# Padded score rows, filler matmuls, a later due time for MLP units and another engine for some subtractions in a fused attention and MLP kernel

## The chip, the cores and the metric

The kernel runs on one core of one Trainium2 chip. The metric is device time in microseconds of a whole execution. The core has a matrix engine (TensorE, PE in the profile, with PEld for its weight loads), a vector engine (VectorE, DVE), a scalar engine (ScalarE, ACT), a general engine (GpSimd, POOL) and a queue that issues the transfers (SyncE, SP).

## What is computed

Attention with a bias of running sums, then two MLPs, all in float32 (B, H, S, D = 4, 8, 576, 64; 2304 tokens of 512 numbers):

```python
scores = q @ k.T / 8 + minimum(-(cum_i - cum_j), 0)   # cum: running sum of relu(s); causal mask
attn = softmax(scores) ; x = attn @ v                 # per batch and head, 576 x 576
h = x @ w_in ; g = h * clip(h + 3, 0, 6) / 6 ; x2 = g @ w_out        # 512 -> 2048 -> 512
m = maximum(maximum(x2 @ w1, x2 @ w2), x2 @ w3) ; out = m @ w_out2   # 512 -> 768 -> 512
```

## The kernel before

Most products are made of three products of float32r numbers: each operand is kept as a rounded high part and a low part (the difference), and `three` (L474 to L476) multiplies high by high, high by low and low by high. Only the first batch's attention is different: its scores and values are multiplied as plain float32, with one instruction in the program that the trace shows as two records.

The order of the work is made in Python before anything is built. `Flow` is a planner: every strand of work is a generator that asks for an engine with a cost in the planner's own microseconds (`mm(n)` is n/2400 + 0.003, and a plain float32 matmul is asked for at `4 * mm(n)`), for a buffer (`Stock`) or for an event. Whoever has the lowest rank gets the engine next, and instructions are issued to the engines' queues in the order in which the planner gave them out. An engine then works in that order on the chip: an instruction that waits holds up all behind it on its queue. After each piece of work that isn't chained, the strand goes on only after a latency (0.2 us for PE, `LATENCY`).

The stages, by the span: the first batch's attention (8 heads; the 128-row blocks of queries 0 and 1 of every head first, then blocks 2 to 4), about 10 to 125 us; the other three batches' attention up to about 355 us, with units of the first MLP between (`hidden1`: `ps_h<-x,w`; `reduce1`: `ps_x<-gt,w`); the rest of the first MLP up to about 684 us; the three products of the second MLP (`ps_j`) up to 882 us; and the last product (`ps_o`) from 882 us to the end. Before the first scores, `setup` (L556) makes `WARM` = 20 matmuls of the 128 x 128 identity with itself.

A block of scores of the first batch goes through `slot` (L806): a matmul whose contracted rows are the 64 numbers of a head and one row for the bias, `tiles[0][0:D + 1, ...]`, so 65 rows; VectorE adds the mask and takes the minimum (L853); ScalarE takes the exponential (L861); TensorE transposes (L883, `pt`); ScalarE copies (L392); and `average` (L915, `px`) multiplies by the 64 columns of the values. The tiles `qt` and `kt` are three pairs of buffers, set up in `staged` (L627 to L635), where GpSimd writes ones into two rows.

The first MLP's unit for a stretch of tokens starts when its `x` is there: for the first batch when it is made, for the others when the transfer that `load_xs` (L1027 to L1043) issues has landed by the planner's reckoning. `hidden1` asks with a rank behind all of attention, so its units fill places that are left.

In the last stage each of 84 right-hand operands (7 combinations of 12 sets) is made of a combination (VectorE, L1183), a rounding to the high part (ScalarE or VectorE, L367, L369) and a subtraction for the low part (L373), which the planner gives to GpSimd or VectorE, whichever takes it first: `hidden_form` (L1544) calls `split_form` (L1177), and that `minus`. The planner treats VectorE and GpSimd operations on SBUF alone as exclusive of each other (`Held`).

Of the kernel before, what the change touches and what calls it, by code (L numbers as in the profile page):

```python
# [9 lines left out]
F32 = mybir.dt.float32  # L10
# [25 lines left out]
NG2 = 3 * NJ // 2  # L36
NG3 = NJ // 2
KEPT = 2
WARM = 20
ORDER = 0  # L40
MOE = 160
AFTER = 8
TINYS = 10
NDM = 1
AFTER_FIRST = 5
AHEAD, BEHIND, PREP = 0, 10, 4
# [70 lines left out]
class Flow:  # L117
    LATENCY = {"PE": 0.2, "DVE": 0.13, "ACT": 0.15, "POOL": 0.08, "SP": 0.0}

    def __init__(self):  # L120
        self.agenda, self.n, self.now = [], 0, 0.0
        self.free = {e: 0.0 for e in self.LATENCY}
        self.ready = {e: [] for e in self.LATENCY}
        self.dma = 0.0
        self.port = 0.0
        self.cur = None
        self.live = set()

# [51 lines left out]
    def dispatch(self, engine):  # L180
        ready = self.ready[engine]
        while ready and self.free[engine] <= self.now + 1e-9:
            passed, chosen = [], None
            while ready and chosen is None:
                one = heapq.heappop(ready)
                if one[5]:
                    continue
                if isinstance(one[3], Held) and self.port > self.now + 1e-9:
                    passed.append(one)
                else:  # L190
                    chosen = one
            for one in passed:
                heapq.heappush(ready, one)
            if chosen is None:
                return
            _, _, th, cost, chained, taken = chosen
            taken.append(engine)
            self.free[engine] = self.now + cost
            if isinstance(cost, Held):
                self.port = self.now + cost  # L200
                for other in ("DVE", "POOL"):
                    if other != engine:
                        self.at(self.port, lambda other=other: self.dispatch(other), ORDER)
            later = 0.0 if chained else self.LATENCY[engine]
            th.t = self.now + cost + later
            self.at(self.free[engine], lambda: self.dispatch(engine), ORDER)
            self.step(th, engine)

    def landing(self, nbytes):
        ev = Event(self)  # L210
# [79 lines left out]
def attn_moe_moe2(ctx, tc, q, k, v, s, w_in, w_out, w1, w2, w3, w_out2, out):  # L290
# [262 lines left out]
    attention_done = event()  # L553
    finished = [0]

    def setup():  # L556
        make_identity(nc, ident)
        pool.memset(above, 0.0)
# [68 lines left out]
    def staged(z, first=False):  # L627
        if (z, first) not in joined:
            joined[z, first] = qt, kt = tuple(
                qp.tile([P, 2, S], F32 if first else F32R, tag=f"{t}{z}", name=t, bufs=1)  # L630
                for t in ("qt", "kt")
            )
            yield "POOL", pool1(2 * S)
            pool.memset((qt if first else qt.bitcast(F32))[D:D + 2], 1.0)
        return joined[z, first]  # L635

    def first_pairs():
# [168 lines left out]
    def slot(i, item, tiny):  # L806
# [5 lines left out]
        if soon:  # L812
            z, *tiles = yield early[part_of(b, c), p]
            o = c * P - UCUT[part_of(b, c)][0]
            passes = [(tiles[0][0:D + 1, j, o:o + n], tiles[1][0:D + 1, j])]
        else:
            passes = [(lhs[:, qs], rhs) for lhs, rhs in (yield h.ready)]
        w = min(S, (c + 1) * P)
# [208 lines left out]
    def load_xs():  # L1027
        for z in range(2):
            for u in range(NU):
# [10 lines left out]
                        x[:, :, cc], x_d[b][:, cc, :, cs].rearrange("l p t -> p l t"), 8 * P * n  # L1040
                    )
                yield d
                x_ready[z, u].set((x, xi))  # L1043

    def hidden1():
        for z in range(2):
# [127 lines left out]
    XFS, TMP, MF = (stock() for _ in range(3))  # L1174
    STAGE = {n: stock() for n in RIGHT.values()}

    def split_form(hi, src, lo, n):  # L1177
        yield from rounded(hi, src, n, ACT + DVE)
        yield from minus(lo, src, hi.bitcast(F32), n, POOL + DVE)

    def combined(dst, a, b_, op, n):
        yield "DVE", held2(n)
# [360 lines left out]

    def hidden_form(t, name, g, items, raw):  # L1544
        f, home = items[name]
        yield from split_form(f[:, 0], raw, f[:, 1], U1)
        right_ready[t, name, g].set((f, home))

    turn2 = [event() for _ in range(2 * NUNIT + 1)]
# [177 lines left out]
    flow.start(-20, cumulate())  # L1727
    flow.start(-10, first_pairs())
    flow.start(0, issue_slots())
    for f in range(NA):  # L1730
        flow.start(WI_PRIO + WI_STEP * f, decode(w_in[f], W, ("i", f)))
    flow.start(40, late_weights())
# [70 lines left out]
```

## Time and profile before

| | us |
|---|---|
| median of 3 runs | 961.94 |
| the three runs | 958.25, 962.2, 961.94 |
| the profiled execution (one of the three) | 962.2 |
| its span in the trace | 960.4 |
| mean granted clock of TensorE, as a share of 2.4 GHz | 0.961 |

The profile is one execution, taken by the hardware profiler. A row of busy tenths divides the span into 40 equal slices of 24 us; PEclk gives TensorE's granted clock in the same slices in tenths of 2.4 GHz, so that 5 is 1.2 GHz. A row of a group of instructions gives line, engine, operation, what is written and read, shapes (for a matmul the weights as rows*columns, then the moving operand), count, busy time, mean duration, and the engine's idle time just before with what ended it. The ends of matmuls are modelled, so two durations that follow each other can overlap; the spacing of starts is the surer number.

### The profile page before, as it was taken

What the parts mean: (1) busy time and instruction counts of PE and PEld (TensorE: products, weight loads), DVE (VectorE), ACT (ScalarE), POOL (GpSimd) and SP (SyncE); (2) the same over time, 40 slices, a digit from 0 to 9 for tenths busy, and PEclk for the clock granted to TensorE, in tenths of its full rate; (3) what the DMA queues carried; (4) which work ended last, traced back from release to release, by engine and by line L of the source; (5) the groups of instructions that cost most, each with busy time, mean ns of one, the idle gap of its engine ahead of it and who ended that gap; (6) DMA issues with size and microseconds to landing.
All of it is one profiled execution on the core that took longest, in us unless ns stands there. A gap on an engine that the chain in (4) does not pass through costs nothing. (4 is left out here: it accounts for less than half of the span.)

```text
span 960.4 us, 18805 instructions
## 1 busy us (share of the span) xinstructions
PE 937.8 (98%) x6520; PEld 864.7 (90%) x6520; DVE 663.4 (69%) x1606; ACT 477.1 (50%) x1215; POOL 354.3 (37%) x452
## 2 busy tenths in 40 slices
PE   8999999999999999999999999999999999999998
PEld 5545579998999999999999999999999999999888
DVE  5567457778888846885577787762857576666874
ACT  4444577867887745664344444442314232323442
POOL 3353544545645223545253454452000000023552
PEclk7558999999999999999999999999999999999999
DMA  7734376789778326664559688848742121374442
GB/s 200 204 89 113 103 171 163 201 211 252 205 191 229 103 99 218 190 213 135 166 204 322 217 286 298 299 153 283 264 139 63 55 70 36 108 265 122 149 124 74
DMA packets 94878, 167.79 MB, mean 175 GB/s; under 512 B 10144, under 2 KB 60840, under 8 KB 94784
## 3 DMA queue, kind: packets, MB, share of 16 engines
q1 hardware_dynamic: 94784, 166.60, 57.4%
q8 instruction: 51, 0.84, 0.4%
q14 instruction: 43, 0.35, 0.1%
HBM read 96.13 MB, written 49.17 MB: 151 GB/s over the span
## 5 line engine op out<-in xcount | busy, mean ns | idle before, releaser
L474 PE MATMUL ps_h<-x,w 128*128 128x320 f32 (+1 forms) x512 | 159.1, 311 | 4.6 <-DVE g L1075 2.5
L474 PE MATMUL ps_x<-gt,w 128*128 128x320 f32 (+1 forms) x512 | 154.4, 302 | 2.3 <-DVE xf L1150 1.6
L373 POOL TENSOR_TENSOR gt<-g,gt 128x256 fp32r<-128x256 f32 (+1 forms) x107 | 86.9, 812 | 176.5 <-ACT gt L367 175.6
L475 PE MATMUL ps_h<-x,w 128*128 128x320 f32 (+1 forms) x512 | 151.4, 296 | 0.0
L476 PE MATMUL ps_h<-x,w 128*128 128x320 f32 (+1 forms) x512 | 151.2, 295 | 0.0
L475 PE MATMUL ps_x<-gt,w 128*128 128x320 f32 (+1 forms) x512 | 150.7, 294 | 0.0
L476 PE MATMUL ps_x<-gt,w 128*128 128x320 f32 (+1 forms) x512 | 150.5, 294 | 0.0
L475 PE MATMUL ps_j<-xf,wf 128*128 128x288 f32 x432 | 127.9, 296 | 0.0
L476 PE MATMUL ps_j<-xf,wf 128*128 128x288 f32 x432 | 127.6, 295 | 0.0
L474 PE MATMUL ps_j<-xf,wf 128*128 128x288 f32 x432 | 127.5, 295 | 0.0
L832 PE MATMUL ps_s<-kt,qt 66*64 66x288 f32 (+14 forms) x384 | 115.4, 399 | 3.9 <-DMA kt<-c 2.8
L861 ACT ACTIVATE e<-e,tiny 128x384 f32<-128x384 f32 (+4 forms) x160 | 96.0, 600 | 38.5 <-DVE tiny L853 37.2
L1071 ACT ACTIVATE u<-ps_h,half 128x256 f32<-128x256 f32 (+1 forms) x128 | 63.8, 498 | 99.3 <-PE ps_h L476 98.5
L474 PEld LDWEIGHTS ps_h<-x,w 128*128 128x128 f32 x512 | 97.2, 190 | 14.7 <-issue 7.3
L853 DVE CUSTOM_DVE_ANT_0 e<-ps_s,above 128x384 f32<-128x384 f32 (+4 forms) x160 | 76.3, 479 | 44.5 <-PE ps_s L832 42.2
L373 POOL TENSOR_TENSOR mh<-mr,mh 128x288 fp32r<-128x288 f32 x36 | 32.2, 902 | 193.8 <-DVE mh L369 160.4
L1075 DVE SCALAR_TENSOR_TENSOR g<-u,ps_h 128x256 f32<-128x256 f32 (+1 forms) x128 | 57.6, 450 | 62.3 <-ACT u L1071 58.6
L474 PEld LDWEIGHTS ps_x<-gt,w 128*128 128x128 f32 x512 | 96.8, 189 | 3.8 <-DVE xf L1150 1.2
L475 PEld LDWEIGHTS ps_h<-x,w 128*128 128x128 f32 x512 | 97.3, 190 | 0.1
L476 PEld LDWEIGHTS ps_h<-x,w 128*128 128x128 f32 x512 | 97.0, 189 | 0.0
L475 PEld LDWEIGHTS ps_x<-gt,w 128*128 128x128 f32 x512 | 96.4, 188 | 0.1
L476 PEld LDWEIGHTS ps_x<-gt,w 128*128 128x128 f32 x512 | 96.3, 188 | 0.0
(159 smaller groups left out, 2220.2 us busy)
## 6 DMA issues: line engine op xcount, KB each, us to landing
f_d<-wf SPq DMA_DIRECT2D x30, 512.0 KB
wf<-f_d SPq DMA_DIRECT2D x30, 512.0 KB
raw<-in_w_out_dram SPq DMA_DIRECT2D x22, 512.0 KB
kt<-kb SPq DMA_DIRECT2D x72, 144.0 KB
raw<-in_w_dram SPq DMA_DIRECT2D x18, 512.0 KB
x<-x_d SPq DMA_DIRECT2D x28, 320.0 KB
raw<-in_w_in_dram SPq DMA_DIRECT2D x16, 512.0 KB
x<-x_d SPq DMA_DIRECT2D x28, 256.0 KB
```

Source lines behind the costliest of these rows:

```text
L373: (pool if e == "POOL" else vec).tensor_tensor(out=dst, in0=a, in1=b_, op=ALU.subtract)
L474: pe.matmul(ps, lhsT=wh, rhs=xh, start=first, stop=False, skip_group_check=again)
L475: pe.matmul(ps, lhsT=wh, rhs=xl, start=False, stop=False, skip_group_check=again)
L476: pe.matmul(ps, lhsT=wl, rhs=xh, start=False, stop=last, skip_group_check=again)
L832: pe.matmul(o, lhsT=lhs, rhs=rhs[:, lo:hi], start=(x == 0), stop=(x == len(passes) - 1),)
L853: vec.tensor_tensor_reduce(out=e[:n, lo:hi], in0=ps[:n, 0:hi - lo], in1=above[:n, shift + lo:shift + hi], scale=-0.125, scalar=m0, op0=ALU ...
L861: act.activation(e[:n, :w], e[:n, :w], AF.Exp, bias=m0, scale=-1.0, accum_out=r,)
L1071: act.activation(ut, ps, AF.Relu, bias=half, scale=1.0 / 6.0)
L1075: vec.scalar_tensor_tensor(out=g, in0=ut, scalar=1.0, in1=ps, op0=ALU.min, op1=ALU.mult)
```

## The change

- Scores of the first batch: both operands are taken over all 128 rows. The rows behind the 64 numbers are zeroed when the tile pair is first used (VectorE writes `kt[D:]`, GpSimd writes `qt[D:]`), and the row of ones is written after that (one row in place of two).
- `WARM` goes from 20 to 34.
- A new strand `keep_warm` runs until the planner's clock is at 60 us. Whenever the planner has PE at work for less than 0.8 of its last 3.4 us, it asks for PE behind everyone else and issues one 128 x 128 float32 matmul of the identity with itself into whichever of the score, transpose or value PSUM buffers has most free places; the result is not used. Otherwise it looks again 0.2 us later.
- `x_ready` for tokens whose `x` is loaded is set 2.5 us later in the planner, so `hidden1` asks later for those units.
- `hidden_form` gives its subtractions to VectorE alone.

```diff
--- before.py
+++ after.py
@@ -36,11 +36,12 @@
 NG2 = 3 * NJ // 2
 NG3 = NJ // 2
 KEPT = 2
-WARM = 20
+WARM = 34
 ORDER = 0
 MOE = 160
 AFTER = 8
 TINYS = 10
+FILL, FILL_UNTIL, WINDOW = 0.8, 60, 3.4
 NDM = 1
 AFTER_FIRST = 5
 AHEAD, BEHIND, PREP = 0, 10, 4
@@ -123,6 +124,7 @@
         self.ready = {e: [] for e in self.LATENCY}
         self.dma = 0.0
         self.port = 0.0
+        self.worked = []
         self.cur = None
         self.live = set()
 
@@ -196,6 +198,8 @@
             _, _, th, cost, chained, taken = chosen
             taken.append(engine)
             self.free[engine] = self.now + cost
+            if engine == "PE":
+                self.worked.append((self.now, self.now + cost))
             if isinstance(cost, Held):
                 self.port = self.now + cost
                 for other in ("DVE", "POOL"):
@@ -205,6 +209,14 @@
             th.t = self.now + cost + later
             self.at(self.free[engine], lambda: self.dispatch(engine), ORDER)
             self.step(th, engine)
+
+    def activity(self, span):
+        lo, done = self.now - span, 0.0
+        for a, b in reversed(self.worked):
+            if b <= lo:
+                break
+            done += b - max(a, lo)
+        return done / span
 
     def landing(self, nbytes):
         ev = Event(self)
@@ -553,6 +565,22 @@
     attention_done = event()
     finished = [0]
 
+    def keep_warm():
+        while flow.now < FILL_UNTIL:
+            free = max((T, S_, V), key=lambda st: len(st.items))
+            if free.items and flow.activity(WINDOW) < FILL:
+                item = free.items.pop(0)
+                yield "PE", 4 * mm(P), False, 1e9
+                pe.matmul(
+                    make(item, [P, 512], F32, "idle")[:, 0:P], lhsT=ident, rhs=ident,
+                    start=True, stop=True,
+                )
+                free.put(item)
+            else:
+                later = event()
+                later.set(at=flow.now + 0.2)
+                yield later
+
     def setup():
         make_identity(nc, ident)
         pool.memset(above, 0.0)
@@ -630,8 +658,13 @@
                 qp.tile([P, 2, S], F32 if first else F32R, tag=f"{t}{z}", name=t, bufs=1)
                 for t in ("qt", "kt")
             )
+            if first:
+                yield "DVE", held1(2 * S)
+                vec.memset(kt[D:], 0.0)
+                yield "POOL", pool1(2 * S)
+                pool.memset(qt[D:], 0.0)
             yield "POOL", pool1(2 * S)
-            pool.memset((qt if first else qt.bitcast(F32))[D:D + 2], 1.0)
+            pool.memset(qt[D:D + 1] if first else qt.bitcast(F32)[D:D + 2], 1.0)
         return joined[z, first]
 
     def first_pairs():
@@ -812,7 +845,7 @@
         if soon:
             z, *tiles = yield early[part_of(b, c), p]
             o = c * P - UCUT[part_of(b, c)][0]
-            passes = [(tiles[0][0:D + 1, j, o:o + n], tiles[1][0:D + 1, j])]
+            passes = [(tiles[0][:, j, o:o + n], tiles[1][:, j])]
         else:
             passes = [(lhs[:, qs], rhs) for lhs, rhs in (yield h.ready)]
         w = min(S, (c + 1) * P)
@@ -1040,7 +1073,7 @@
                         x[:, :, cc], x_d[b][:, cc, :, cs].rearrange("l p t -> p l t"), 8 * P * n
                     )
                 yield d
-                x_ready[z, u].set((x, xi))
+                x_ready[z, u].set((x, xi), at=flow.cur.t + 2.5)
 
     def hidden1():
         for z in range(2):
@@ -1174,9 +1207,9 @@
     XFS, TMP, MF = (stock() for _ in range(3))
     STAGE = {n: stock() for n in RIGHT.values()}
 
-    def split_form(hi, src, lo, n):
+    def split_form(hi, src, lo, n, engines=POOL + DVE):
         yield from rounded(hi, src, n, ACT + DVE)
-        yield from minus(lo, src, hi.bitcast(F32), n, POOL + DVE)
+        yield from minus(lo, src, hi.bitcast(F32), n, engines)
 
     def combined(dst, a, b_, op, n):
         yield "DVE", held2(n)
@@ -1543,7 +1576,7 @@
 
     def hidden_form(t, name, g, items, raw):
         f, home = items[name]
-        yield from split_form(f[:, 0], raw, f[:, 1], U1)
+        yield from split_form(f[:, 0], raw, f[:, 1], U1, DVE)
         right_ready[t, name, g].set((f, home))
 
     turn2 = [event() for _ in range(2 * NUNIT + 1)]
@@ -1727,6 +1760,7 @@
     flow.start(-20, cumulate())
     flow.start(-10, first_pairs())
     flow.start(0, issue_slots())
+    flow.start(NS, keep_warm())
     for f in range(NA):
         flow.start(WI_PRIO + WI_STEP * f, decode(w_in[f], W, ("i", f)))
     flow.start(40, late_weights())
```

## Rows read from the trace of the kernel before

**Rows 1.** The page: span, busy time, and the clock granted in 40 slices

```profile
span 960.4 us, 18805 instructions
...
PE 937.8 (98%) x6520; PEld 864.7 (90%) x6520; DVE 663.4 (69%) x1606; ACT 477.1 (50%) x1215; POOL 354.3 (37%) x452
...
PEclk7558999999999999999999999999999999999999
```

**Rows 2.** TensorE's instructions in order: start, us, what, [idle before it]

```profile
1.35 6.39 PE L574 MATMUL warm<-ident 128*128 128x128 f32 x40 [1.35 <-POOL ident masks.py:199]
10.52 0.89 PE L832 MATMUL ps_s<-kt,qt 65*128 65x128 f32 x4 [2.78 <-DMA kt<-c]
12.01 1.65 PE L832 MATMUL ps_s<-kt,qt 65*128 65x128 f32 x4 [0.60 <-DVE tiny L853]
```

**Rows 3.** Stretches: length, PE PEld DVE ACT POOL busy (x instructions), clock, DMA share, GB/s

```profile
11.50:12.00 0.50, 0.00 (x0) 0.00 (x0) 0.50 (x4) 0.01 (x1) 0.43 (x1) 0.69 1.46 164
12.00:62.00 50.00, 49.48 (x135) 27.44 (x136) 29.17 (x92) 26.27 (x83) 19.19 (x28) 0.50 0.66 179
62.00:79.70 17.70, 17.70 (x45) 8.60 (x44) 9.04 (x25) 6.26 (x15) 4.63 (x7) 0.50 0.29 81
79.70:84.00 4.30, 4.30 (x19) 1.84 (x18) 2.69 (x5) 2.03 (x6) 2.13 (x3) 0.97 0.40 122
84.00:120.00 36.00, 36.00 (x176) 20.28 (x177) 21.47 (x61) 20.20 (x52) 18.30 (x24) 1.00 0.45 118
882.00:946.00 64.00, 59.48 (x426) 57.97 (x425) 52.95 (x102) 29.96 (x84) 37.20 (x43) 0.97 0.44 135
```

**Rows 4.** TensorE's instructions in order, shortly before the clock rises

```profile
77.53 1.70 PE L883 MATMUL pt<-ident,e 128*128 128x128 f32 x7
79.16 1.13 PE L915 MATMUL px<-e2p,vf 128*64 128x320 f32 x2
```

**Rows 5.** TensorE's instructions in order, from one MLP unit to the next, later

```profile
102.14 0.28 PE L476 MATMUL ps_h<-x,w 128*128 128x256 f32 x1
...
103.57 0.93 PE L883 MATMUL pt<-ident,e 128*128 128x128 f32 x7
104.43 0.75 PE L915 MATMUL px<-e2p,vf 128*64 128x320 f32 x2
...
109.30 0.39 PE L474 MATMUL ps_h<-x,w 128*128 128x256 f32 x1
```

**Rows 6.** VectorE by line, 10 to 84 us: busy, mean ns, idle before, releaser

```profile
L853 DVE CUSTOM_DVE_ANT_0 e<-ps_s,above 128x128 f32<-128x128 f32 (+4 forms) x28 | 12.5, 450 | 21.9 <-PE ps_s L832 21.8
```

**Rows 7.** Stretches around a fall of the clock in the later batches

```profile
216.00:220.00 4.00, 2.96 (x22) 2.20 (x20) 3.87 (x13) 3.82 (x11) 4.00 (x6) 0.99 0.92 220
220.00:224.00 4.00, 3.84 (x17) 3.66 (x18) 2.66 (x12) 2.35 (x7) 0.34 (x1) 0.59 0.93 257
```

**Rows 8.** The warm-up line alone, two records to a matmul: stretches of 1 us

```profile
4.00:5.00 1.00, 1.00 (x7) 1.00 (x6) 1.00 0.90 254
5.00:6.00 1.00, 1.00 (x11) 1.00 (x10) 1.00 1.06 315
```

**Rows 9.** Line 634, whole span: duration ns min/median/max, first and last start

```profile
L634 POOL MEMSET qt<- x6: 1051/1051/1057, 2.4 to 119.1; 2x1152 f32 x6
```

**Rows 10.** TensorE's waits over the whole span: us in total, times, longest

```profile
PE ps_o L475 <- DVE mh L373: 3.4, 3, 1.5
...
PE ps_h L474 <- DVE g L1075: 2.5, 3, 1.4
...
PE ps_o L475 <- POOL mh L373: 1.2, 3, 0.5
```

**Rows 11.** Lines 373 and 1183, 836 to 950 us: duration ns min/median/max

```profile
L373 POOL TENSOR_TENSOR mh<-mr,mh x36: 802/832/1117, 839.1 to 944.8; 128x288 fp32r<-128x288 f32 x36
...
L373 DVE TENSOR_TENSOR mh<-mh x17: 445/451/1071, 891.9 to 943.4; 128x288 fp32r<-128x288 f32 x17
L1183 DVE TENSOR_TENSOR mr<-mr,mh x12: 445/752/1067, 840.0 to 937.0; 128x288 f32<-128x288 f32 x12
```

## The prediction

> **What bounds the kernel now.** The page first [rows 1]: TensorE works in 98% of the span, and the line of the granted clock has one long hole, slices 2 to 4, with 5 where all later slices have 9. So the end is set by TensorE's work and by the clock at which it is done, and any other engine matters where TensorE waits for it. The hole is the first batch's attention, and the stretches give its edges [rows 3]: the clock falls from 2.4 to 1.2 GHz between 11.5 and 12.0 us, is 0.50 in all of 12.0 to 79.7, and 0.97 and 1.00 after that. In those 67.7 us TensorE is busy for 49.48 + 17.70 = 67.2 us: it is slow, not idle. What came before the fall stands in its order of work [rows 2]: 20 warm-up matmuls to 7.74 us, 2.78 us of waiting for the transfer of the bias row, one pair of scores, 0.60 us of waiting for VectorE. That TensorE is what the others wait for in this stretch shows on VectorE [rows 6]: before its score line it was idle 21.9 us from 10 to 84 us, 21.8 of them for TensorE's scores. The rest of the span is full at 2.4 GHz; two late places matter for the last two edits: waits in the last stage and for MLP units [rows 10].
>
> **What a release of the clock is worth.** The spacing of starts gives the ratio of the two levels for the same work. Seven transposes take 79.16 - 77.53 = 1.63 us at 1.2 GHz [rows 4] and 104.43 - 103.57 = 0.86 at 2.4 [rows 5], 1.9 to 1. So the 67.2 us are 35.4 us of work at 2.4 GHz. With 0.9 before 12 us [rows 2] and 4.3 from 79.7 to 84.0 [rows 3], everything that TensorE has done by 84.0 us is W = 40.6 us, from the first score on.
>
> **Does the clock stay up?** Once up, the first batch's own mix keeps it up: from 102.14 to 109.30 us no MLP matmul runs, only the 65-row scores, transposes and 64-column values [rows 5], and the clock of that stretch is 1.00 in the row of 84 to 120 us [rows 3]. The same mix did not raise it in 12 to 62 us. So what must be avoided is the fall, and the fall had idle time before it. WARM gives 14 more matmuls, 28 records; at the rate of the fifth us, 11 records in 1 us [rows 8], that is 2.6 us, so the warm-up ends at 7.74 + 2.6 = 10.3, at the first score's 10.52. The padded rows cost no TensorE time that I can see in a row; the nearest are scores of 128 rows in the later batches, in a float format of their own. For them there is one sign more: in the later batches, after a fall at about 220 us, the clock is back within 4 us [rows 7], not after 67. The zeroing adds three GpSimd operations of about 1.05 us [rows 9] and three on VectorE, before the first score where both have gaps, but for the third pair, which puts about 1 us in front of weight subtractions that nothing waits for yet; 0, with 1 us as the other end.
>
> [...]
>
> **The fillers.** `keep_warm` issues at most one per 0.425 us of the planner's time (0.225 for the matmul, 0.2 latency, both in the code). It starts at the planner's 0, where no real matmul is due, and the planner knows nothing of the warm-up. The first score comes at 10.5 us in the trace, which bounds them at 25; the planner's transfers and VectorE costs are shorter than the traced ones, so I take 18. A filler is two records, 0.19 us at the rate above: 3.4 us behind the warm-up, and the first score starts at 10.3 + 3.4 = 13.7 instead of 10.5 (ends 10.5 and 15.1). This isn't all lost, since the clock holds through it, and scores of pairs 1 to 3 come later than pair 0's. After that, fillers stand where the planner has TensorE below 0.8: mostly the first group (12 to 37 us in the trace, half of it at 2.4 GHz), where no MLP unit can fill. Half of the 47 places in 20 us gives 24, D = 4.6 us. Ends: 0, and 117 places in the remaining 50 us of the planner, 22 us. On the chip they cost only where TensorE isn't waiting anyway; with plain float32 values slower than the planner's cost, most will not fall in idle time. Each waits for the last reader of its buffer, and the scores and transposes behind it on TensorE's queue wait with it.
>
> **What is late next.** VectorE has 29.17 + 9.04 + 2.69 = 40.9 us of work from 12 to 84 [rows 3]; in 13.7 to 61 that would be 0.87 of the time, against 0.60 from 84 to 120. So some waits for it will show: I = 3 us (ends 0 and 11).
>
> **The sum for the first batch.** 13.7 + 40.6 + 4.6 + 3 = 61.9 for the point that is now at 84.0: 22.1 us less.
>
> **MLP units held back.** The longest wait for a unit is on VectorE's gate (2.5 us in three) [rows 10], that is, on a PSUM buffer coming free and not on a loaded x. So no wait that the trace shows is removed; a shift of the order is worth 0, with 2 us on either side. Behind a unit that is issued later wait only its own gate, the GpSimd subtraction and `reduce1`.
>
> **Low halves on VectorE.** In 882 to 946 us TensorE is idle 64 - 59.48 = 4.5 us [rows 3], nearly all waits for these low halves, 3.4 on VectorE's and 1.2 on GpSimd's [rows 10]. There are 43 on GpSimd in this stretch. Alone a VectorE one takes 0.45 us and a GpSimd one 0.80; beside each other VectorE's combinations take up to 1.07 [rows 11]. VectorE's 102 operations take 52.95 us now; at 0.45 and less they would take 46 or less, so moving 43 in at 0.37 to 0.45 adds 16 to 19 and gives back 7 to 12: 57 to 65 us of work in 64. I take 58, a few waits gone: -1 us. Ends: -6 (all waits and a short fall of the clock there, 0.97), and +7 if VectorE becomes the bound and its sums behind PSUM wait.
>
> [...]
>
> **The forecast.** 962.2 (of which 1.8 lie outside the span) - 22.1 - 1 = 939; this execution is within 0.3 us of the median. About 0.5%, 4.8 us, is what a measurement of this kernel can tell from no change.
>
> **The rivals.**
> 1. *The clock holds only in part.* Waits for transfers or VectorE let it fall as at 216 to 224 us, where TensorE was busy 2.96 of 4 us and the next 4 us ran at 0.59 [rows 7]. If 12 of the 40.6 us of work run at 1.2 GHz, that adds 0.9 x 12 = 11: 950 (944 to 959). For it: VectorE at 0.87. Against: TensorE starts 3 us late, so work has piled up before it.
> 2. *The last stage turns to VectorE.* The clock does as forecast, but VectorE has more work than TensorE in 882 to 946: +7 us in place of -1: 947. For it: up to 65 us in 64. Against: GpSimd no longer stretches its operations.
> 3. *The clock doesn't hold; slower.* If it falls at the first scores all the same and rises only with the MLP units, the fillers are pure load at half the clock: first score 3.2 us later, and 24 fillers at 0.33 us (six or seven records in 1 us, the slower rate in rows 8), 8 us: 962 + 11 = 973. It decides by the clock between 14 and 60 us: with fewer than about a quarter of that work at 2.4 GHz, the fillers cost more than it gives.
> 4. *The change doesn't do what it says:* padding and fillers neither raise nor hold it, but the fillers fall in idle time: 960 to 964. I count this with the upper edge of 1 and the lower edge of 3.
>
> **How the numbers follow.** The forecast 0.56 (own range 931 to 947), rival 1 0.20, rival 2 0.09, rival 3 0.15. Faster by over 0.5%: 0.56 + 0.09 + 0.16 of rival 1 = 0.81; within it 0.04 of rival 1 and 0.03 of rival 3 = 0.07; slower 0.12. The range of 929 to 957 holds all but the ends of the forecast (0.53), rival 2 and 0.17 of rival 1: 0.79.
>
> **What would show it.** Right: granted clock 1.00 from 1 to 60 us, the first score near 14 us, the work of 12 to 62 us done by about 47, GpSimd idle after 836 us, VectorE's combinations at 0.45. Wrong: 0.50 in any slice after the first, TensorE waiting for `tiny` or for a transfer in 14 to 45 us, fillers that wait for a PSUM reader, waits for low halves over 4.6 us.

## The result, and the profile after

The changed kernel takes 944.55 us (median of 4 runs, 943.45 to 946.17) against 960.2 for the kernel before (4 runs, 958.25 to 962.2): a ratio of 0.984, 95% interval 0.981 to 0.987. That is 15.7 us less; the forecast was 939, so 5.5 us too low, inside the range. The profiled execution has a span of 941.7 us, 18.7 less than [rows 1].

The page after, in the lines that answer to [rows 1], with GpSimd's row added:

```profile
span 941.7 us, 18963 instructions
...
PE 922.3 (98%) x6630; PEld 859.8 (91%) x6630; DVE 671.7 (71%) x1661; ACT 479.7 (51%) x1220; POOL 307.0 (33%) x398
...
POOL 4365354654744125554253444442000000000000
PEclk9999999999999999999999999999999999999999
```

The hole in the clock is gone, slice 1 included, and GpSimd is idle in the last 12 slices. The stretches, as in [rows 3] and with the same columns:

```profile
12.00:36.00 24.00, 22.72 (x139) 16.73 (x137) 16.12 (x53) 14.40 (x50) 10.49 (x14) 1.00 0.68 187
...
42.00:48.00 6.00, 6.00 (x22) 2.83 (x20) 4.83 (x13) 3.25 (x10) 2.21 (x4) 0.73 1.04 257
48.00:62.00 14.00, 13.78 (x60) 6.52 (x59) 10.68 (x30) 9.50 (x24) 10.70 (x15) 1.00 0.73 207
868.00:932.00 64.00, 62.17 (x459) 60.79 (x458) 56.84 (x151) 30.13 (x84) 0.00 (x0) 1.00 0.46 144
```

One short dip is left: the granted clock is 0.73 from 42 to 48 us. The last line is the last product's first 64 us, which before were 882 to 946. TensorE's order around the start, answering to [rows 2]: start, duration, what, and the wait before it:

```profile
10.67 4.73 PE L574 MATMUL idle<-ident 128*128 128x128 f32 x40
15.24 0.92 PE L865 MATMUL ps_s<-kt,qt 128*128 128x128 f32 x4
...
23.70 0.89 PE L865 MATMUL ps_s<-kt,qt 128*128 128x128 f32 x4 [0.62 <-DMA kt<-in_k_dram]
...
41.07 0.88 PE L865 MATMUL ps_s<-kt,qt 128*128 128x384 f32 x2 [2.10 <-DMA kt<-in_k_dram]
```

Twenty fillers (40 records) stand ahead of the first score, which comes at 15.24 us instead of 10.52. The dip follows the 2.10 us wait for a head's `k`. The ratio of the two levels in [rows 4] and [rows 5] is borne out by the pair of value matmuls over 320 columns. Before, one that starts at 71.28 us is followed at 72.54; after, one at 65.06 is followed at 65.74: 1.26 us at a granted clock of 0.50 against 0.68 at 1.00. The traces give the clock as a share of the full one; what the prediction calls 2.4 and 1.2 GHz are its shares of 1.00 and 0.50.

Where the 18.7 us come from is read from where the same work stands in both traces. The table has a line for each kernel of this study. "Mark" is the time at which TensorE has streamed as many matmul columns (records times moving columns, twice for plain float32, without warm-up and fillers) as the kernel before has at 84.0 us, the point that the prediction used. "Middle" runs from the last attention score to the first matmul of the last product, "last product" from its first to its last matmul start. All are from each kernel's profiled execution, and two executions of the changed kernel differ by 1.4 us in the mark. The median, the number of runs and the mean clock are beside them. The kernels ran on several chips, on which the kernel before has medians of 957.6 to 960.2 us; so they are best compared by the ratio, which is to the kernel before on the same chip.

| kernel | mark | last score | middle | last product | span | median (runs) | ratio to before | clock |
|---|---|---|---|---|---|---|---|---|
| before | 84.0 | 336.8 | 545.1 | 74.6 | 960.4 | 960.2 (4) | 1 | 0.961 |
| after | 70.3 | 323.9 | 544.1 | 70.2 | 941.7 | 944.55 (4) | 0.984 | 0.998 |
| after, once more | 68.9 | 322.4 | 544.5 | 70.7 | 941.1 | 943.43 (4) | 0.985 | 1.00 |
| pad_only | 66.0 | 320.1 | 557.4 | 73.3 | 954.4 | 957.04 (10) | 0.999 | 0.989 |
| warm34_only | 78.1 | 330.5 | 546.8 | 73.4 | 954.6 | 954.29 (10) | 0.993 | 0.973 |
| rows_65 | 72.0 | 326.9 | 549.3 | 70.9 | 950.6 | 951.59 (10) | 0.994 | 0.987 |
| no_fillers | 67.4 | 320.3 | 553.6 | 69.4 | 946.8 | 945.99 (4) | 0.987 | 0.989 |
| fill_after_first_score | 71.6 | 327.1 | 547.1 | 69.5 | 947.2 | 947.24 (4) | 0.989 | 0.990 |
| zeros_in_setup | 66.3 | 321.4 | 551.6 | 69.3 | 945.8 | 946.35 (4) | 0.987 | 0.996 |
| zeros_in_setup_late | 60.7 | 312.9 | 548.9 | 69.2 | 934.5 | 936.16 (4) | 0.977 | 0.996 |
| zeros_in_setup_no_fillers | 61.7 | 313.5 | 544.1 | 69.4 | 930.5 | 933.29 (4) | 0.973 | 0.998 |
| no_hold | 69.8 | 326.4 | 547.7 | 70.4 | 948.0 | 950.07 (6) | 0.991 | 1.00 |
| lows_on_both | 70.6 | 325.6 | 544.2 | 73.5 | 947.3 | 949.41 (4) | 0.991 | 0.998 |
| lows_only | 79.3 | 332.6 | 545.2 | 69.5 | 950.9 | 952.6 (10) | 0.991 | 0.969 |

So after against before: the first batch gives 13.7 us (84.0 to 70.3), the last product 4.4, and the rest of the span 0.6. About 1.2 of the 4.4 go with a dip of the clock in the last product of this one execution (0.97 in [rows 3]): `pad_only`, `warm34_only` and `lows_on_both`, with the old last stage and no dip there, need 73.3 to 73.5 us.

The last stage, in the lines that answer to [rows 10] and [rows 11]: first TensorE's waits from 860 to 945 us (us in total, times, longest), then VectorE's lines from 800 to 930 us (busy, mean ns, idle before):

```profile
PE ps_o L487 <- DVE mh L385: 1.8, 4, 0.9
```

```profile
L385 DVE TENSOR_TENSOR mh<-mr,mh 128x288 fp32r<-128x288 f32 x36 | 15.7, 452 | 0.1
...
L1216 DVE TENSOR_TENSOR mr<-mh 128x288 f32<-128x288 f32 x18 | 8.1, 453 | 0.9 <-DMA mh<-m_d 0.9
```

Waits for low halves fall from 4.6 to 1.8 us, and subtractions and combinations take 0.45 us each.

### The profile page after: what moved, and what is told of

It reads as the page before. It is cut to its first block, busy times and chain, and to the rows that moved or that the text cites. A ratio compares the mean times of both kernels' runs of the same rounds, so it can differ in the third digit from the quotient of the medians.

```text
span 941.7 us, 18963 instructions
## 1 busy us (share of the span) xinstructions
PE 922.3 (98%) x6630; PEld 859.8 (91%) x6630; DVE 671.7 (71%) x1661; ACT 479.7 (51%) x1220; POOL 307.0 (33%) x398
## 4 chain that ended last, share of the span: by engine, by line
PE 79%; DMA 8%; DVE 6%; issue 2%; SPq 1%; ACT 1%; POOL 1%; DVEq 0%; POOLq 0%; ACTq 0%
PE ps_j L487 7%; PE ps_j L488 7%; PE ps_j L486 7%; PE ps_s L865 7%; PE ps_h L486 6%; PE ps_x L486 5%; PE ps_h L487 5%; PE ps_h L488 5%; PE ps_x L487 5%; PE ps_x L488 5%; PE pt L916 5%; PE px L955 3%; PE px L948 3%; PE ps_o L487 2%; DMA raw<-in_w_out_dram 2%
## 5 line engine op out<-in xcount | busy, mean ns | idle before, releaser
L486 PEld LDWEIGHTS ps_h<-x,w 128*128 128x128 f32 x512 | 96.7, 189 | 11.9 <-issue 5.5
L865 PE MATMUL ps_s<-kt,qt 128*64 128x288 f32 (+9 forms) x384 | 102.8, 362 | 2.9 <-DMA kt<-in_k_dram 2.7
L886 DVE CUSTOM_DVE_ANT_0 e<-ps_s,above 128x384 f32<-128x384 f32 (+4 forms) x160 | 75.9, 477 | 30.1 <-PE ps_s L865 27.7
L379 ACT ACTIVATE gt<-g 128x256 fp32r<-128x256 f32 (+1 forms) x128 | 56.6, 442 | 56.7 <-DVE g L1108 54.9
```

Of the source, the lines that this page charges most:

```text
L379: act.activation(dst, src, AF.Copy)
L486: pe.matmul(ps, lhsT=wh, rhs=xh, start=first, stop=False, skip_group_check=again)
L865: pe.matmul(o, lhsT=lhs, rhs=rhs[:, lo:hi], start=(x == 0), stop=(x == len(passes) - 1),)
L886: vec.tensor_tensor_reduce(out=e[:n, lo:hi], in0=ps[:n, 0:hi - lo], in1=above[:n, shift + lo:shift + hi], scale=-0.125, scalar=m0, op0=ALU ...
```

## The experiments

Each edit is against the changed kernel unless it says before.

### Which part holds the clock: padding alone, warm-up alone, fillers without padding, padding without fillers

`pad_only` is the kernel before with the padded rows and their zeroing, nothing else.

> The kernel before with the padded rows and their zeroing, and nothing else: 20 warm-up matmuls, no fillers. Theory 1: padded rows let the clock come back by itself. It falls near 11.7 us as before, is back before 24 us, and is low for 5 to 20 us in all before the MLP units; time 945 to 951. Theory 2: padding needs the warm-up: 0.50 until MLP units come, 956 to 962.

Measured: 957.04 us, ratio 0.9985 (0.9958 to 1.0012): no change that can be measured. Theory 1 has the clock about right and the time wrong. The first batch is done faster than in the full change, with the mark at 66.0. Its stretches from 12 us on (columns as in [rows 3]):

```profile
12.00:18.00 6.00, 5.05 (x15) 2.81 (x16) 5.18 (x16) 3.71 (x14) 3.13 (x4) 0.57 0.74 202
18.00:24.00 6.00, 5.47 (x17) 3.50 (x17) 3.51 (x12) 2.98 (x11) 3.56 (x4) 0.50 0.51 144
24.00:30.00 6.00, 5.25 (x23) 2.76 (x21) 5.18 (x16) 3.11 (x11) 1.42 (x2) 0.79 0.80 218
...
36.00:42.00 6.00, 6.00 (x23) 2.98 (x24) 5.18 (x16) 5.12 (x17) 2.02 (x3) 0.94 1.06 310
```

The clock falls as in the kernel before, and then comes back in 24 to 42 us, with TensorE busy 5.25 us of 6 from 24 to 30; in 12 to 62 us before it was busy 49.48 of 50 [rows 3], and the clock stayed at 0.50. The mean clocks of all runs agree. Twice (1 - mean clock) times the span is an estimate of the time at 0.50, as if the clock were else at 1.00: 8 to 25 us in the ten runs of `pad_only`, 38 to 79 in all runs of the kernel before. So this edit brings the clock back earlier. That the rows do it, and not the new order that the zeroing gives the planner, is argued: 65 rows with the zeroing kept, which would leave the order as it is here, were not run.

The 18.0 us gained by the mark are 16.7 at the last score. Then 12.3 are lost in the middle, for the most part on waits of TensorE from 340 to 700 us (us in total, times, longest); first `pad_only`, then the changed kernel:

```profile
PE ps_h L474 <- DVE g L1080: 7.5, 10, 1.6
PE ps_x L474 <- DVE g L1080: 3.7, 4, 1.5
PE ps_h L474 <- ACT part L392: 2.6, 3, 1.7
```

```profile
PE ps_h L486 <- DVE g L1108: 2.7, 3, 1.5
PE ps_h L486 <- ACT part L404: 1.4, 2, 1.2
...
PE ps_x L486 <- DVE g L1108: 0.7, 2, 0.4
```

One of the ten, in order of time on its engines:

```profile
551.90 0.69 DVE L430 SCALAR_TENSOR_TENSOR ps_m<-ps_m,raw 128x512 f32<-128x512 f32 x1
552.62 0.69 DVE L436 TENSOR_SCALAR wr<-ps_m 128x512 uint32<-128x512 uint32 x1
553.23 0.41 DVE L1080 SCALAR_TENSOR_TENSOR g<-u,ps_h 128x256 f32<-128x256 f32 x1
...
553.69 0.38 PE L474 MATMUL ps_h<-x,w 128*128 128x256 f32 x1 [1.63 <-DVE g L1080]
```

The gate `g` stands in VectorE's order behind the steps of decoding a weight, and TensorE's next unit waits for it. The decoding comes between because the planner's order put it there; any edit makes it plan anew. VectorE's work is nearly the same, 216.5 us from 340 to 640 us in `pad_only`, 213.7 before and 214.6 after, but TensorE is idle 300 - 282.05 = 18.0 us there, against 6.9 and 6.1. So the order is what differs. Why this plan was worse than that one is not shown.

`warm34_only` is the kernel before with `WARM` = 34.

> The kernel before with 34 warm-up matmuls in place of 20 and nothing else. Theory 1: the idle 2.78 us ahead of the first score were what let the clock fall; bridged, it holds as it does at 102 to 109 us, for at least the first group, and the time is 940 to 948. Theory 2: the waits of the first group (0.6 us and more) let it fall within 10 us of the first score, it stays at 0.50 until the MLP units, and the time is 957 to 962.

Measured: 954.29 us, ratio 0.9933 (0.9899 to 0.9967), with single runs from 943.6 to 959.2: theory 2's fall, at a time below its range. In the profiled one the clock is 1.00 from 12 to 18 us, 0.56 from 18 to 24 and 0.50 until 66: the longer warm-up moves the fall by some 7 us, and the clock stays down for 51. In the fastest run it can't have: its mean clock of 0.994 leaves 11 us at 0.50 by that estimate.

`rows_65` is the changed kernel with 65 rows and without the zeroing.

> The changed kernel with scores of 65 rows again and without the zeroing. Theory 1 (the fillers hold the clock, and rows don't matter while it is up): clock 1.00 to 39 us as with padded rows; after the wait for pair 0's second group near 40 us it falls and, with 65 rows, stays at 0.50 until MLP units come at 55 us or later: 15 to 25 us of half clock, 7 to 11 us more than the changed kernel, 951 to 955. Theory 2 (rows matter nowhere): within 2 us of the changed kernel. Theory 3 (rows carry it all): clock near 0.50 from the first scores on, 965 or more.

Measured: 951.59 us, ratio 0.9936 (0.9903 to 0.9969). Its stretches:

```profile
18.00:24.00 6.00, 5.01 (x27) 2.97 (x25) 4.64 (x17) 5.31 (x19) 2.67 (x5) 1.00 0.94 197
24.00:30.00 6.00, 5.55 (x20) 4.10 (x21) 4.03 (x14) 3.24 (x13) 0.88 (x2) 0.59 1.09 179
...
36.00:42.00 6.00, 6.00 (x15) 2.58 (x13) 3.14 (x11) 3.56 (x12) 3.13 (x5) 0.50 1.06 280
...
48.00:54.00 6.00, 6.00 (x29) 3.38 (x27) 5.05 (x13) 3.69 (x10) 3.66 (x6) 0.92 0.13 44
```

The clock is up to 24 us; then it falls, and with TensorE busy 5.55 us of 6 and after that all the time it stays down until about 49. It then comes back with 65 rows, before the first MLP unit at 60.3 us. The time is theory 1's; the fall comes some 14 us before the place that it named. The mark, 72.0, is 12.0 us earlier than before without any padding.

`no_fillers` leaves `keep_warm` out:

```diff
-    flow.start(NS, keep_warm())
```

> The changed kernel without the fillers; 34 warm-up matmuls, padded rows, the later due time and the low halves on VectorE stay. Theory 1 (fillers hold the clock): the clock falls to 0.50 within the first group, in the stretch of 12 to 40 us, for 5 us or more; with padded rows it is back before the MLP units; first MLP unit at 50 to 56 us, time 941 to 950. Theory 2 (the warm-up and the padded rows are enough): clock over 0.95 in 12 to 60 us, first MLP unit near 48, time 937 to 940. If the clock stays at 0.50 until the MLP units, 955 or more, the fillers are the whole effect.

Measured: 945.99 us, ratio 0.9868 (0.9827 to 0.9909), not told apart from the changed kernel's 0.984, and as theory 1 has it. Its mark is earlier, 67.4 against 70.3, although the clock falls twice (0.56 in 18 to 24 us, 0.62 in 48 to 54) and comes back each time. With padded rows, then, the fillers save no time in the first batch. What makes the end equal is the middle, 553.6 against 544.1 us.

### Why the first batch gave 13.7 us and not 22.1

In the changed kernel pair 1's transfers start late. SP's own queue (start, duration of issue):

```profile
11.55 0.43 SPq L358 DMA_DIRECT2D cum_d<-ch  x1
18.06 0.34 SPq L358 DMA_DIRECT2D raw<-in_w_in_dram  x1
18.45 0.66 SPq L358 DMA_DIRECT2D qt<-in_q_dram  x1
19.15 0.61 SPq L358 DMA_DIRECT2D kt<-in_k_dram  x1
```

and VectorE and GpSimd in the same time:

```profile
9.36 1.02 DVE L663 MEMSET kt<- 64x1152 f32 x1 [0.30 <-issue]
...
11.74 0.69 DVE L448 TENSOR_SCALAR da<-ps_m 128x512 uint32<-128x512 uint32 x1
15.66 0.29 DVE L886 CUSTOM_DVE_ANT_0 e<-ps_s,above 128x128 f32<-128x128 f32 x1 [3.23 <-PE ps_s L865]
...
17.36 0.68 DVE L458 SCALAR_TENSOR_TENSOR da<-raw,ps_m 128x512 uint32<-128x512 uint32 x1
```

```profile
10.71 1.06 POOL L665 MEMSET qt<- 64x1152 f32 x1
11.82 1.05 POOL L667 MEMSET qt<- 1x1152 f32 x1
```

The zeroing keeps pair 1's loads back until they stand, in SP's order, behind a transfer of raw weights into a buffer that VectorE's decoding must free (L458, done at 18.04 us). That decoding stands behind the first score's reduction (L886, which waits 3.23 us), and that score stands behind twenty fillers. Pair 1's `q` and `k` go out at 18.45 and 19.15 us; in the kernel before it was 9.44 and 10.89. It takes both edits: with fillers and no zeroing (`rows_65`) they go out at 9.10 and 10.53, and raw weights at 17.69 hold pair 2; with zeroing and no fillers (`no_fillers`) at 12.03 and 15.09. Four more kernels take this apart.

`fill_after_first_score` starts the fillers when the planner has given out the first score:

```diff
+    first_scored = event()
     def keep_warm():
+        yield first_scored
         while flow.now < FILL_UNTIL:
...
             parts.append((bank, ps, lo, hi))
+            if i == 0:
+                first_scored.set()
```

> The changed kernel, but the fillers begin only when the planner has given out the first score. Theory 1: the 20 fillers ahead of the first score (10.67 to 15.24 us) hold up VectorE's queue behind the first score's reduction, the weight decoding behind that, and the SP queue behind its transfer, so that pair 1's operands are asked for at 18.45 us. Then the first score starts at 10.6 to 11, pair 1's q transfer is issued before 14, the first MLP unit comes near 49 in place of 54.8 us, and the kernel takes 4 to 6 us less than the changed one: 938 to 940. Theory 2: what was lost against the forecast is only the fixed cost of each plain float32 matmul, which doesn't halve with the clock; then the first score is earlier, but the first MLP unit stays within 2 us of 54.8 and the time within 2 us of 944.

Measured: 947.24 us, ratio 0.9889 (0.9856 to 0.9923). The first score comes at 11.9 us, 3.3 earlier, and nothing is gained: raw weights still stand between pair 1's `q` (11.96) and `k` (15.86), TensorE waits 2.21 us for that `k` at 21.19, the clock is 0.76 in 18 to 24 us and 0.68 and 0.75 in 36 to 48. Neither theory came: theory 1 had the first score and the issue of `q` right, but not the gain, and the first MLP unit comes at 61.9 us. For theory 2's cost that doesn't halve with the clock, the seven transposes of [rows 4] and [rows 5] give an estimate: 1.63 us at 0.50 and 0.86 at 1.00 are 2 x 0.86 - 1.63 = 0.09 us for the seven. Moving the fillers alone was the wrong cure.

`zeros_in_setup` does the zeroing in `setup`, before anything is planned, for all three pairs of buffers:

```diff
+        for z in range(3):
+            joined[z, True] = qt, kt = tuple(
+                qp.tile([P, 2, S], F32, tag=f"{t}{z}", name=t, bufs=1) for t in ("qt", "kt")
+            )
+            pool.memset(qt[D:], 1.0)
+            vec.memset(kt[D:], 0.0)
```

> The changed kernel with the three tile pairs filled in setup (one GpSimd operation of ones for each qt, one VectorE operation of zeros for each kt, none of them in the planner's reckoning), fillers unchanged. Theory 1: in the changed kernel the zeroing puts pair 1's transfers behind a weight transfer on SP that waits for VectorE's decoding; without it pair 1's q and k are issued before 13 us, no wait for a kt transfer in 15 to 30 us is left, and the time is 2 to 5 us under the changed kernel. Theory 2: the fillers ahead of the first score hold the same queue up all the same (pair 1 near 18 us); time within 1.5 us of the changed kernel.

Measured: 946.35 us, ratio 0.9868 (0.9832 to 0.9904), no gain beside 943.43 for the changed kernel on the same chip. Pair 1's `q` is now issued at 8.49 us, as theory 1 has it, but the fillers still push the first score, to 15.9, and the same chain now holds pair 3: raw weights at 17.32, then its `q` at 18.98.

`zeros_in_setup_late` has both edits.

> As zeros_in_setup, and the fillers begin only when the planner has given out the first score. Theory 1: first score at 10.6 to 12, pair 1's q and k issued before 13 us, its first score before 17, clock over 0.95 from 1 to 36 us, first MLP unit before 50 us, the fastest of the set: 5 to 9 us under the changed kernel. Theory 2: TensorE then runs out of scores in the first group and the clock falls as in the kernel whose fillers began late (0.76 in 18 to 24 us): within 2 us of the changed kernel.

Measured: 936.16 us, ratio 0.9769 (0.9735 to 0.9802), 7 us less than the changed kernel on the same chip, as theory 1 has it. The first score comes at 10.6 us, pair 3's `q` at 14.37, the mark at 60.7. Only five fillers are left, since the planner has TensorE at work.

`zeros_in_setup_no_fillers` has the zeroing in `setup` and no `keep_warm`.

> The changed kernel with the tile pairs filled in setup and no fillers at all. Theory 1: the longer warm-up and the padded rows do the work, and the fillers are no part of it (the version whose fillers began late issued 5): any fall of the clock in 12 to 60 us is over within 8 us, time 934 to 939, within 2 us of that version. Theory 2: those 5 fillers between the first scores keep the clock up; without them it falls before 24 us and the time is 940 to 946.

Measured: 933.29 us (932.29 to 934.3), ratio 0.9733 (0.9705 to 0.9761): the fastest kernel of the study, with theory 1's clock and a time a little under its range. SP's queue and the stretches (columns as in [rows 3]):

```profile
8.50 0.65 SPq L358 DMA_DIRECT2D qt<-in_q_dram  x1
9.19 0.60 SPq L358 DMA_DIRECT2D kt<-in_k_dram  x1
...
13.93 0.37 SPq L358 DMA_DIRECT2D raw<-in_w_in_dram  x1
```

```profile
12.00:36.00 24.00, 20.17 (x95) 11.69 (x95) 19.39 (x66) 15.27 (x56) 10.68 (x17) 1.00 1.01 243
36.00:42.00 6.00, 3.93 (x15) 2.00 (x15) 4.58 (x11) 4.86 (x13) 4.34 (x7) 0.73 0.80 218
42.00:62.00 20.00, 18.47 (x84) 9.70 (x83) 17.47 (x42) 11.67 (x28) 11.20 (x17) 1.00 0.52 155
```

TensorE is idle 3.8 us of the 24 from 12 to 36 us without a filler in it, and the clock is 1.00. When heads arrive early enough and their scores have 128 rows, fillers gain nothing here.

The mark of four kernels can be taken apart: the first score's start; TensorE's idle time from there to the mark; the time of fillers by their records; the loss by the clock, which is (1 - mean clock) x length x 2 x 0.9 / 1.9, with the 1.9 to 1 of [rows 4] and [rows 5]; and W, what is left of TensorE's busy time, its work at a clock of 1.00.

| | first score | W | clock | idle | fillers behind it | mark |
|---|---|---|---|---|---|---|
| forecast | 13.7 | 40.6 | 0 | 3 | 4.6 | 61.9 |
| after | 15.2 | 41.9 | 1.6 | 3.6 | 8.0 | 70.3 |
| no_fillers | 10.8 | 41.9 | 6.4 | 8.3 | 0 | 67.4 |
| pad_only | 10.5 | 41.8 | 7.9 | 5.8 | 0 | 66.0 |
| zeros_in_setup_no_fillers | 10.6 | 42.2 | 1.4 | 7.5 | 0 | 61.7 |

W is the same in these four. The account is rougher where fillers stand alone between scores: for `fill_after_first_score` it gives 11.1 us of fillers and a W of 37.7, so the records of such fillers seem to count time that is partly the scores'. The late loads of pair 1 (in `pad_only` too, where raw weights at 15.35 us stand between its `q` at 12.16 and its `k` at 15.74) are paid for in one of two ways: without fillers by a clock that falls in the wait (6.4 and 7.9 us), with them by the fillers themselves (4.6 us ahead of the first score, 8.0 behind it, of which 8.3 - 3.6 = 4.7 stand, by the two kernels' idle times, where TensorE is idle without them). With the loads early (`zeros_in_setup_no_fillers`) neither is paid.

### The two late edits

`no_hold` takes the 2.5 us out of `load_xs`:

```diff
-                x_ready[z, u].set((x, xi), at=flow.cur.t + 2.5)
+                x_ready[z, u].set((x, xi))
```

> The changed kernel with the later due time of the MLP units taken back. Theory 1: no wait for a loaded x was there to be removed: within 2.5 us of the changed kernel (0.983 to 0.988 of before), no TensorE wait for a transfer of x. Theory 2: the stages run closer together now and units wait for their x: such waits of 2 us or more between 100 and 340 us, and 3 to 6 us slower than the changed kernel.

Measured: 950.07 us, ratio 0.9907 (0.9877 to 0.9937), against 0.984 and 0.985 for the changed kernel on other chips: by the ratios the hold is worth some 6 us. The slowdown is theory 2's, but the waits that it named are not there. The mark is the same (69.8); from there to the last score it takes 256.6 us against 253.6, and the middle 547.7 against 544.1. TensorE's waits from 340 to 700 us:

```profile
PE ps_h L486 <- DVE g L1108: 4.2, 4, 1.4
PE ps_x L486 <- DVE g L1108: 1.7, 2, 1.6
```

For VectorE's gates it waits 5.9 us instead of 3.4. No wait for a loaded `x` stands there, and one of 0.8 us before 340 us. So it is not shown that the hold works by keeping units from starting before their `x` has landed. What is shown is that it leads the planner to another order, and that this order has fewer waits.

`lows_on_both` lets GpSimd take subtractions of the last stage again:

```diff
-        yield from split_form(f[:, 0], raw, f[:, 1], U1, DVE)
+        yield from split_form(f[:, 0], raw, f[:, 1], U1)
```

> The changed kernel with the last stage's subtractions on GpSimd or VectorE again. Theory 1: the 4 us that the last stage gained come from this edit: the last product takes 74 to 75 us from its first to its last matmul again (70.3 in the changed kernel), VectorE's combinations take up to 1.07 us, and the whole is 3 to 5 us slower than the changed kernel. Theory 2: they come from another order of the stage before, and the last product takes 70 to 72 us.

Measured: 949.41 us (948.48 to 950.75), ratio 0.991 (0.9874 to 0.9945), beside 943.43 for the changed kernel on the same chip, 6 us more. The last product is 73.5 us long instead of 70.7, so 2.8 of them are there, as theory 1 has it. The profiled mark is 1.7 later, in a part that the edit doesn't touch; the rest is not traced. VectorE's combinations from 800 to 945 us, then TensorE's waits from 860 to 945:

```profile
L1216 DVE TENSOR_TENSOR mr<-mr,mh 128x288 f32<-128x288 f32 x12 | 9.1, 758 | 1.0 <-POOL mh L385 1.0
...
L1216 DVE TENSOR_TENSOR mm<-mh 128x288 f32<-128x288 f32 x6 | 3.7, 624 | 0.0
```

```profile
PE ps_o L487 <- DVE mh L385: 3.4, 3, 1.5
PE ps_o L487 <- POOL mh L385: 1.5, 3, 0.7
```

The means are 758 and 624 ns here, and 452 to 454 with GpSimd idle. In the kernel before, from 836 to 946 us, all 29 VectorE operations on two SBUF operands that take over 0.52 us (up to 1.07) overlap a GpSimd operation; of the 75 shorter ones 20 do. What makes them longer is not shown beyond that.

`lows_only` is the kernel before with this edit alone.

> The kernel before with the last stage's subtractions on VectorE alone and nothing else. Theory 1: GpSimd's subtractions held up VectorE's combinations; the last product's matmuls take 70 to 71 us from first to last in place of 74.7, all VectorE combinations take 0.45 us, and the whole is 3 to 6 us faster than before. Theory 2: VectorE becomes the bound: 75 us or more and the same time or slower.

Measured: 952.6 us, ratio 0.9913 (0.9884 to 0.9942), 7.5 less than before. Not all of this is the edit. Runs of the kernel before differ by their mean clock: on this chip those at 0.961 took 962.8 and 963.5 us, those at 0.971 took 954.6 and 955.6. `lows_only` took 957.1 at 0.961, and 950.1, 950.8 and 952.6 at 0.971. At the same clock the edit is worth 4 to 6 us. Its last product takes 69.5 us against 74.6, or against 73.3 to 73.5 where the old stage has no dip: 4 to 5 us, much as theory 1 has it.

### The changed kernel once more

`changed_again` is the changed kernel itself.

> The changed kernel as it is, beside the others of this call: ratio to the kernel before 0.980 to 0.988, the clock over 0.95 from 1 to 36 us, pair 1's q transfer issued near 18.4 us, the first MLP unit at 54 to 55 us, the last product's TensorE work over about 70.3 us.

Measured: 943.43 us (942.71 to 946.95), ratio 0.9852 (0.9818 to 0.9886). That is within its expectation, but for the first MLP unit at 53.5 us. In this profile the longest wait for a `k` is 1.2 us, and the first batch has no dip of the clock. So the dip of the first profile, with its 2.10 us wait, is a matter of the single run, and its cost (1.6 us in the table above) is not in every execution.

## Why the prediction held, and where its steps failed

*What bounds, and what the clock is worth: right.* TensorE's work at its clock sets the end. W, the work up to the mark, was put at 40.6 us, and is 41.9 in the changed kernel (the table above).

*Does the clock stay up: right in the result, wrong in the reason.* The prediction held that once up, the first batch's mix keeps it up, and that only the fall must be avoided; it gave the padded rows "one sign more". In `rows_65`, with fillers and warm-up but 65 rows, the clock falls to 0.59 in 24 to 30 us, behind a stretch in which TensorE is busy 5.01 us of 6, and is at 0.50 for some 24 us. In `pad_only` and `no_fillers`, with 128 rows, it falls too, but is back within 14 us. So a fall need not be avoided if the clock comes back early: their marks, 66.0 and 67.4, are ahead of the changed kernel's. Padding alone brings the mark from 84.0 to 66.0 us, warm-up and fillers without it to 72.0, all together to 70.3: the parts do not add, and once the rows are padded the fillers are not needed.

*The zeroing at 0, with 1 us as the other end: the step that failed.* The durations were right (1.02, 1.06 and 1.05 us) and both engines did have gaps. What was left out is a queue that the zeroing is put ahead of: SP's. Pair 1's loads came to stand behind a transfer that waits for VectorE. From `no_fillers` to `zeros_in_setup_no_fillers`, which differ in where the rows are filled and in the order planned around it, the mark goes from 67.4 to 61.7: 5.7 us. A cost by duration on the engine that executes it was the wrong account; the step decided when the next transfers are issued.

*The fillers: counts nearly right, sizes too small.* 20 before the first score, 20 between it and the mark and one at 122 us, for 18 and 24. Those ahead took 4.57 / 20 = 0.23 us each instead of 0.19. The 0.19 was a misreading: the 11 records of [rows 8] count those that only overlap an end of the microsecond, and the 40 records of the fillers ahead come at 0.114 us each. The warm-up, priced at the same rate, ends at 10.67 instead of 10.3. So the first score is 1.5 us later than forecast. The fillers behind it, which mostly stand alone and not in a row, fill 8.0 us by the records instead of 4.6. The prediction's "This isn't all lost, since the clock holds through it" is right by the table, but without them and with the loads early the clock costs 1.4 us, not 6.4; the rest is the zeroing's doing.

*What is late next: right in size, wrong in place.* I was put at 3 us, of waits for VectorE; it is 3.6, of which 2.7 are for transfers of `k` and 0.2 for `tiny`. Without fillers in the gaps it is 5.8 to 8.3. Rival 1's doubt, a fall of the clock after a wait for a transfer, came at a size of 1.6 us instead of 11.

So the 8.4 us that the first batch fell short of the forecast are 1.5 of the first score, 3.4 of fillers, 1.3 of W, 1.6 of the clock and 0.6 of waits.

*MLP units held back at 0, with 2 on either side: wrong,* some 6 us of gain against the same kernel without it. It was argued from the waits that the old order has. The edit makes the planner order everything anew, and the price is in the new order's waits, which no row of the trace before shows. That the rest of the span still came out at 0.6, near the forecast 0, means that the other edits' new order cost about as much as this one gained: that is luck.

*Low halves at -1: too small.* It is -4.4 us in the changed kernel, and -2.8 and -5.1 in the two experiments. VectorE's work was forecast well, 58 us in 64 against 56.84. What was undersized is what that frees: the idle time of the stretch falls from 4.5 to 64 - 62.17 = 1.8 us, 2.7 less. The clock of the stretch rises from 0.97 to 1.00, which by the same account is 0.03 x 64 x 0.95 = 1.8; but that the edit removes this dip is not shown, since `lows_on_both` has the old waits and no dip. The prediction had both only in its better end.

*The rivals.* Rivals 2, 3 and 4 did not come: the waits in the last stage fell, the clock held, and it moved the time. Rival 1's price was not paid: the mean clock is 0.998.

The misses have opposite signs: against the profiled execution's 943.51 us, 8.4 us too much was expected of the first batch, and 3.4 too little of the last stage and 0.6 of the rest. That is why 939 came near, and that they cancel by half is luck.

## What to carry to other kernels

When an edit adds an operation that has to come before a transfer, cost it by the transfers it delays and by what they then queue behind, not by its own microseconds. When a stage runs at half the clock, try the cheapest change to the matmuls themselves (here 63 zero rows, with the mark at 66.0 us in place of 84.0) before adding matmuls that do nothing. And where a planner makes the order, judge an edit by stage marks in the trace as well as by the total: here 18 us gained in one stage by the padding alone were given back by two thirds in a later one by a new order.

## What the runs showed of the hardware

After a fall to 0.50 in the first batch the granted clock came back later with 65-row scores than with 128-row ones. With 65 rows it stayed down for 68 us before, 51 in `warm34_only` and 24 in `rows_65`, with TensorE busy nearly all the time (49.48 us of 50 before). In the last it came back ahead of the first MLP unit: 0.92 in 48 to 54 us, the unit at 60.3. In `lows_only` the mean clock of the profiled execution, 0.969, stands for 59 us at 0.50 by the estimate above. In the ten profiled executions with 128 rows no fall of the first batch lasted over 14 us, whatever the order of the work; the longest is that of `pad_only`, 0.57, 0.50 and 0.79 in the three stretches from 12 to 30 us. There, with TensorE busy 5.25 and 4.71 us of 6 in 24 to 30 and 30 to 36 us, the clock went from 0.50 in 18 to 24 us to 0.94 in 36 to 42. Two kernels of the same order that differ in the rows alone were not compared.

How long the clock stays down differs from run to run of one kernel, by its mean clock: `warm34_only` took 943.6 us in a run at 0.994 and 956.4 in one at 0.973. Runs of a kernel in which it hardly is down lie closer: the four of the changed kernel, at 0.998 and 1.00, within 2.7 us of each other, the six of `no_hold`, at 0.998 and 1.00, within 4.8.

VectorE's operations on two SBUF operands of 128 x 288 numbers took 0.45 us with GpSimd idle (450 to 459 ns in the changed kernel's last stage), and up to 1.07 beside GpSimd's subtractions [rows 11].
